# Spectral filter and two expert layers on one core: the image of x moved to partitions 0 to 46 and 64 to 110, with a rewritten start of the program

## The chip, the cores and the metric

The kernel runs on one core of a Trainium2 chip. The metric is the device time of one execution in microseconds (us); the time before is the median of three executions. The engines are PE (matrix products; its weight loads are listed as PEld), DVE and ACT (elementwise work), POOL (here mostly transfers and small copies) and SP (only issues transfers). A row that ends in q, such as SPq, is an engine's issue of a transfer. Each engine runs its own instructions strictly in program order.

## What is computed

```python
X = np.fft.rfft(x, axis=1)                 # x: 2 x 3008 x 256
Yr = Xr @ w_r - Xi @ w_i + b_r
Yi = Xr @ w_i + Xi @ w_r + b_i
Y  = soft_threshold(Yr, 0.01) + 1j * soft_threshold(Yi, 0.01)
y  = np.fft.irfft(Y, n=3008, axis=1)       # then 6016 tokens of 256
h  = y @ w_in;   y  = (h - tanh(h)) @ w_out            # 256 -> 2048 -> 256
h  = y @ w_in2;  out = (h * clip(h + 3, 0, 6) / 6) @ w_out2
```

## The kernel before

The transform of length 3008 = 47 x 64 is done in stages. Stage A (`dft_a`, chunks i = 0 to 15, eight for each batch) multiplies a chunk of x by a small constant matrix `amt`; ACT and DVE write the result back over the chunk (`dft_a_out`), and ACT issues its store to DRAM (`s<-xa` for batch 0, `s<-xb` for batch 1). Batch 0 lies whole in the tile `xa` (views `x0[0]` to `x0[7]`); batch 1 goes through a ring of three tiles `xb` (`x1`), each loaded by SP (`load_x`), used by PE, evicted, stored and then loaded again. Batch 0's first group of frequencies is also copied straight from `xa` into the ring tile `bi_all` by four transfers; the other groups are read back from DRAM (`load_bi`).

Stage B (`dft_b(j)`) multiplies a group of `bi_all` by a group of `bmt` (`load_bm(g)`, four frequencies in each, two used by each `dft_b`). ACT makes a high part `fh` and DVE a low part `fl` (`evict_b_*`). `linear(t)` is 24 PE instructions on `fh` and `fl`; DVE then does bias and threshold (`shrink(t)`: lines 349 to 351), ACT and DVE split the result into `sh` and `sl` (lines 357 and 361), and stage C (`dft_c`) goes back in frequency with the constants `cmH` and `cmL`, which POOL loads (`load_cm`, behind a small copy that waits for its last argument). A loop over t = 0 to 23 interleaves `linear(t)`, `dft_c(t - 2)`, `dft_b(t + 2)` and, while there are chunks left, one `dft_a` of batch 1. The order written in the code is the order that each engine keeps (`manual_schedule`).

The weights of the expert layers come as 64-bit floats (`raw`, three buffers) and are decoded to high and low parts on ACT and DVE by a generator, `w_steps`: each `w_step()` emits a step of it, in turn ACT lines 174 and 175, ACT line 184, DVE lines 177 and 187 with the next load (`w_load`), DVE line 192, DVE line 199, and for half of the weights DVE lines 203, 204 and then 206, 207. Five steps are run ahead of the loop, and six in each iteration from t = 2 to 9, fewer later, until 13 weights are decoded. `A0` is the number of chunks that go through stage A ahead of the loop. The expert layers, which fill the rest of the program, are not touched.

All transfers of SP and ACT share eight completion semaphores, which the tile framework hands out in turn: a transfer is not issued until the one that had its semaphore before it has landed. So at most eight transfers of these two queues are under way.

Of the kernel before, what the change touches and what calls it, by code (L numbers as in the profile page):

```python
# [18 lines left out]
N1 = 47  # L19
# [8 lines left out]
def dft_constants():  # L28
# [44 lines left out]

    am96 = np.zeros((96, 128))
    am96[0:94, 0:96] = am.reshape(94, 96)
    am96[0:94, 96:128] = am.reshape(94, K1, 4)[:, 0:8].transpose(0, 2, 1).reshape(94, 32)
    cm = cm.reshape(128, K1 * 128).astype(f)
# [11 lines left out]
def spectral_moe_kernel(ctx: ExitStack, tc: tile.TileContext, x, w_r, w_i, b_r, b_i,  # L89
# [25 lines left out]
    def split(hi, lo, src, lo_eng=None):  # L115
        act.activation(out=hi, in_=src, func=ACTF.Copy)  # L116
        (lo_eng or dve).tensor_tensor(out=lo, in0=src, in1=hi.bitcast(F32), op=ALU.subtract)  # L117
# [20 lines left out]

    A0 = 9
    NDEC = 13  # L140
# [95 lines left out]
    bias = ca.tile([128, 1, D], F32, name="bias")  # L236
    amt = ca.tile([96, 128], F32, name="amt")
    x1 = [wia.tile([128, 4, D], F32, tag=f"wo{5 + r}", name=f"xb{r}") for r in range(3)]
# [8 lines left out]
    def load_x(i):  # L247
        if i >= 16:
            return
        b, c = divmod(i, 8)  # L250
        if b == 0:
            v = x.rearrange("b s d -> (b s) d")[0:96 * 32].rearrange("(r j) d -> r j d", j=32)
            sp.dma_start(out=x0[c][0:96], in_=v[:, 4 * c:4 * c + 4, :])
        else:
            v = x[b].rearrange("(r j) d -> r j d", j=32)[:, 4 * c:4 * c + 4, :]
            for r0, r1 in ((0, 80), (80, 94)):
                sp.dma_start(out=x1[c % 3][r0:r1], in_=v[r0:r1])

# [5 lines left out]
    def dft_a(i, finish=True):  # L264
        b, c = divmod(i, 8)
        xt = (x1[c % 3] if b else x0[c])[0:96]
        m = 96 if b else 128
# [347 lines left out]
    with tc.manual_schedule():  # L615
# [12 lines left out]
        sp.dma_start(out=amt, in_=am)  # L628
        for i in range(8):
            load_x(i)  # L630
        warm = ca.tile([128, 256], F32, name="warm")
# [4 lines left out]
        for r in range(3):  # L636
            pool.memset(x1[r][64:96], 0.0)
        dve.memset(three, 3.0)
# [5 lines left out]
        load_bm(0)  # L644
        load_x(8)
        w_load()
        for k, w in enumerate((b_r, b_i)):
            sp.dma_start(out=bias[64 * k:64 * k + 64, 0, :],
                         in_=w.rearrange("(o d) -> o d", o=1).broadcast_to([64, D]))
        for i in range(A0):  # L650
            dft_a(i)
            if i == 5:
                for k in range(2):
                    split(lwH[:, k], lwL[:, k], lws[k])
            if i == 7:
                for k in range(GB):
                    sp.dma_start(out=bi_ring[0][:, k, :], in_=xa[96 + k:128:8])
                bi_t[0] = bi_ring[0]
        load_x(9)
        load_bi(1)  # L660
        load_bm(1)
        load_x(10)
        w_load()
        sp.dma_start(out=dmt, in_=dm)
        for _ in range(5):
            w_step()
        wa_cm.__exit__(None, None, None)
        wpool["r"] = ctx.enter_context(tc.tile_pool(name="wr", bufs=1, side="right", reuse_waits="tile"))
        for j in range(2):
            dft_b(j)  # L670
            evict_b_hi(j)
            evict_b_lo(j)
            evict_b_neg(j)
            if j == 0:
                load_cm(0, xf_t[0][0].bitcast(F32)[0:1, 0, 64:65])
        load_bi(2)
        NP = K1
        a_next = A0
        for t in range(NP):
# [21 lines left out]
            for _ in range(3 if t < 10 else 2):  # L701
                if t > 1 and ptr["dec"] < NDEC:
                    w_step()
# [11 lines left out]
            if t % 2 == 0:  # L715
                load_bm(t // 2 + 2)
                load_cm(t // 2 + 1, s_t[t][0].bitcast(F32)[0:1, 0, 0:1])
            load_x(11 + t)
            if t == 0:
# [3 lines left out]
            for _ in range(3 if t < 10 else 1 + t % 2):  # L723
                if t > 1 and ptr["dec"] < NDEC:
                    w_step()
# [124 lines left out]
```

## Time and profile before

| what | value |
|---|---|
| median of 3 executions (lowest, highest) | 1214.83 us (1214.05, 1216.38) |
| the profiled execution: time, span of its records | 1212.14 us, 1210.3 us |
| PE, DVE, ACT, POOL busy share of the span | 98%, 80%, 72%, 13% |
| granted clock of PE, mean | 0.993 |

The profiled execution lies 2.7 us under the median, within 2 us of the fastest run. PE's share is over the whole program; of the first tenth, the stages above, it says little.

### The profile page before, as it was taken

To read this page: it belongs to the slowest core of one execution; us is meant where nothing else is said; L and a number is where in the kernel's file an instruction comes from. 1 tells how busy PE (TensorE), PEld (TensorE's weight loads), DVE (VectorE), ACT (ScalarE), POOL (GpSimd) and SP (SyncE) were. 2 spreads that over 40 slices of the span, in tenths; PEclk is the share of its full clock that TensorE was granted. 3 is DMA by queue.
4 is the path that set the end of the run, shared out by engine and by line. 5 is a ranking of instruction groups with operands and counts; after the bars stand their busy time and mean duration, and the time that the engine had idled before them with its cause. 6 is when DMAs were issued, how large, how long until landed. Compare 5 with 4: busy or idle time off the path is not lost.

```text
span 1210.3 us, 20904 instructions
## 1 busy us (share of the span) xinstructions
PE 1185.4 (98%) x7832; PEld 1164.5 (96%) x7832; DVE 965.6 (80%) x1820; ACT 875.2 (72%) x1827; POOL 157.2 (13%) x162
## 2 busy tenths in 40 slices
PE   7989999999999999999999999999999999999998
PEld 5888989999999999999999999999999999999998
DVE  2589988888988888888777787878787878787875
ACT  2576678777777777777777677777777777776765
POOL 0100000203020110202021402011020202020200
PEclk8899999999999999999999999999999999999999
DMA  9996621112232223120105530101010101010000
GB/s 292 284 308 187 205 87 44 41 70 74 92 105 74 75 75 100 57 82 25 51 1 196 178 111 1 52 1 52 1 52 1 53 1 52 1 29 24 14 14 26
DMA packets 47797, 96.52 MB, mean 80 GB/s; under 512 B 4352, under 2 KB 27488, under 8 KB 47696
## 3 DMA queue, kind: packets, MB, share of 16 engines
q1 hardware_dynamic: 41728, 74.09, 19.2%
q0 software_dynamic: 4032, 14.68, 3.8%
q10 hardware_dynamic: 1936, 6.42, 1.4%
q8 instruction: 61, 1.00, 0.3%
q14 instruction: 40, 0.33, 0.1%
HBM read 58.22 MB, written 36.44 MB: 78 GB/s over the span
## 4 chain that ended last, share of the span: by engine, by line
PE 73%; DVE 11%; ACT 11%; DMA 2%; issue 2%; SPq 0%; ACTq 0%; DVEq 0%
PE acc L122 13%; PE acc L120 13%; PE acc L121 13%; PE al L120 6%; PE al L121 6%; PE al L122 6%; PE be L122 3%; PE be L121 3%; PE be L120 3%; ACT gh L116 3%; DVE g L447 3%; PE ga L405 2%; DVE gl L117 2%; PE ga L121 1%; PE ga L122 1%
## 5 line engine op out<-in xcount | busy, mean ns | idle before, releaser
L117 DVE TENSOR_TENSOR gl<-g,gh 128x376 fp32r<-128x376 f32 x509 | 292.2, 574 | 149.6 <-ACT gh L116 123.2
L116 ACT ACTIVATE gh<-g 128x376 fp32r<-128x376 f32 x509 | 263.4, 517 | 176.7 <-DVE g L450 91.5
L122 PE MATMUL acc<-wo,gl 128*128 128x256 f32 (+1 forms) x768 | 215.9, 281 | 0.0
L121 PE MATMUL acc<-wo,gh 128*128 128x256 f32 (+1 forms) x768 | 215.8, 281 | 0.0
L120 PE MATMUL acc<-wo,gh 128*128 128x256 f32 (+1 forms) x768 | 215.6, 281 | 0.0
L120 PE MATMUL acc<-gh,wo 128*128 128x376 f32 x512 | 173.2, 338 | 0.0
L122 PE MATMUL acc<-gh,wo 128*128 128x376 f32 x512 | 171.0, 334 | 0.0
L121 PE MATMUL acc<-gl,wo 128*128 128x376 f32 x512 | 170.7, 333 | 0.0
L121 PEld LDWEIGHTS acc<-wo,gh 128*128 128x128 f32 (+1 forms) x768 | 143.0, 186 | 0.0
L122 PEld LDWEIGHTS acc<-wo,gl 128*128 128x128 f32 (+1 forms) x768 | 142.9, 186 | 0.0
L120 PEld LDWEIGHTS acc<-wo,gh 128*128 128x128 f32 (+1 forms) x768 | 142.8, 186 | 0.0
L414 POOL TENSOR_TENSOR bmt<-bmt 128x376 f32<-128x376 f32 x60 | 73.4, 1224 | 445.5 <-ACT bmt L407 331.2
L450 DVE SCALAR_TENSOR_TENSOR g<-e,c 128x376 f32<-128x376 f32 x192 | 118.5, 617 | 12.2 <-ACT e L449 7.5
L449 ACT ACTIVATE e<-c,three 128x376 f32<-128x376 f32 x192 | 116.7, 608 | 7.7 <-DVE c L596 7.5
L447 DVE TENSOR_TENSOR g<-c,e 128x376 f32<-128x376 f32 x189 | 114.5, 606 | 5.9 <-ACT e L446 3.4
L430 POOL TENSOR_TENSOR cmL<-bmt,cmH 128x376 fp32r<-128x376 f32 x60 | 64.9, 1082 | 324.8 <-ACT cmH L425 324.8
L446 ACT ACTIVATE e<-c 128x376 f32<-128x376 f32 x189 | 97.6, 516 | 10.0 <-DVE c L596 9.8
L120 PEld LDWEIGHTS acc<-gh,wo 128*128 128x128 f32 x512 | 96.3, 188 | 0.0
L121 PEld LDWEIGHTS acc<-gl,wo 128*128 128x128 f32 x512 | 96.2, 188 | 0.0
L122 PEld LDWEIGHTS acc<-gh,wo 128*128 128x128 f32 x512 | 96.1, 188 | 0.0
L586 ACT ACTIVATE s<-be 128x376 f32<-128x376 f32 x127 | 61.8, 487 | 40.5 <-PE be L122 39.9
L120 PE MATMUL al<-cmH,wi 128*128 128x376 f32 x256 | 87.3, 341 | 2.1 <-ACT s L582 0.3
(173 smaller groups left out, 2831.2 us busy)
## 6 DMA issues: line engine op xcount, KB each, us to landing
raw<-in_moe_w_in_dram SPq DMA_DIRECT2D x16, 512.0 KB, 3.9
raw<-in_moe_w_out_dram SPq DMA_DIRECT2D x16, 512.0 KB, 4.2
w2id<-wout SPq DMA_DIRECT2D x8, 896.0 KB, 4.7
wi<-w2id POOLq DMA_DIRECT2D x8, 896.0 KB, 4.9
y1d<-y SPq DMA_DIRECT2D x32, 188.0 KB, 2.0
bmt<-y1d SPq DMA_DIRECT2D x8, 752.0 KB, 4.5
s<-co SPq DMA_DIRECT2D x23, 256.0 KB, 4.6
bi_all<-s SPq DMA_DIRECT2D x11, 512.0 KB, 5.1
```

The costliest lines, as they stand in the source:

```text
L116: act.activation(out=hi, in_=src, func=ACTF.Copy)
L117: (lo_eng or dve).tensor_tensor(out=lo, in0=src, in1=hi.bitcast(F32), op=ALU.subtract)
L120: pe.matmul(out=out_ap, lhsT=lh, rhs=rh, start=start, stop=False, **kw)
L121: pe.matmul(out=out_ap, lhsT=lh, rhs=rl, start=False, stop=False, **kw)
L122: pe.matmul(out=out_ap, lhsT=ll, rhs=rh, start=False, stop=stop, **kw)
L414: eng.tensor_tensor(out=out, in0=a, in1=b, op=ALU.subtract)
L430: (eng or dve).tensor_tensor(out=l, in0=OPS[nm][0], in1=h.bitcast(F32), op=ALU.subtract)
L446: act.activation(out=e, in_=src, func=ACTF.Tanh)
L447: dve.tensor_tensor(out=g, in0=src, in1=e, op=ALU.subtract)
L449: act.activation(out=e, in_=src, func=ACTF.Relu, bias=three)
L450: dve.scalar_tensor_tensor(out=g, in0=e, scalar=6.0, in1=src, op0=ALU.min, op1=ALU.mult)
L586: act.activation(out=s5, in_=be, func=ACTF.Copy)
```

## The change

x of batch 0 and 1 is laid out by the parity of its 32-row blocks: even blocks on partitions 0 to 46, odd ones on 64 to 110 (a 48th row of each parity is loaded for batch 0 and multiplied by zero rows of the constant). `amt` has 112 rows instead of 96, with zero rows between, and PE contracts over 112 partitions. A chunk of batch 0 is loaded by two transfers of 48 rows instead of one of 96; a chunk of batch 1 by four (32, 15, 32 and 15 rows) instead of two (80 and 14). What lies between must be finite, so DVE clears partitions 32 to 63 of each batch-0 chunk ahead of its load, and POOL clears two pieces of each `xb` tile instead of one.

The start of the program is rewritten: eight chunks instead of nine go through stage A ahead of the loop; on SP's queue the four copies into `bi_all` stand ahead of the bias, chunk 8 and the first raw weight; the split of the two filter matrices comes behind all of stage A; PE gets 11 products of a zero tile (`warm`) between stage A and stage B; no decode step runs ahead of the loop, and six run at t = 1. One chunk more goes through stage A in the loop (t = 0 to 7), and loads of x in the loop begin at t = 1.

```diff
-    A0 = 9
+    A0 = 8
-        if b == 0:
-            v = x.rearrange("b s d -> (b s) d")[0:96 * 32].rearrange("(r j) d -> r j d", j=32)
-            sp.dma_start(out=x0[c][0:96], in_=v[:, 4 * c:4 * c + 4, :])
-        else:
-            v = x[b].rearrange("(r j) d -> r j d", j=32)[:, 4 * c:4 * c + 4, :]
-            for r0, r1 in ((0, 80), (80, 94)):
-                sp.dma_start(out=x1[c % 3][r0:r1], in_=v[r0:r1])
+        v = x.rearrange("b s d -> (b s) d")[SEQ * b:SEQ * b + 64 * (47 if b else 48)]
+        v = v.rearrange("(n q j) d -> q n j d", q=2, j=32)[:, :, 4 * c:4 * c + 4, :]
+        for q in range(2):
+            if b == 0:
+                sp.dma_start(out=x0[c][64 * q:64 * q + 48], in_=v[q])
+                continue
+            for r0, r1 in ((0, 32), (32, 47)):
+                sp.dma_start(out=x1[c % 3][64 * q + r0:64 * q + r1], in_=v[q, r0:r1])
...
         for i in range(8):
+            dve.memset(x0[i][32:64], 0.0)
             load_x(i)
...
-        load_x(8)
-        w_load()
+        for i in range(A0):
+            dft_a(i)
+        for k in range(GB):
+            sp.dma_start(out=bi_ring[0][:, k, :], in_=xa[96 + k:128:8])
+        bi_t[0] = bi_ring[0]
         for k, w in enumerate((b_r, b_i)):
...
-        for i in range(A0):
-            dft_a(i)
-            if i == 5:
-                for k in range(2):
-                    split(lwH[:, k], lwL[:, k], lws[k])
-            if i == 7:
-                for k in range(GB):
-                    sp.dma_start(out=bi_ring[0][:, k, :], in_=xa[96 + k:128:8])
-                bi_t[0] = bi_ring[0]
+        load_x(8)
+        load_bi(1)
+        w_load()
         load_x(9)
-        load_bi(1)
         load_bm(1)
+        sp.dma_start(out=dmt, in_=dm)
         load_x(10)
         w_load()
-        sp.dma_start(out=dmt, in_=dm)
-        for _ in range(5):
-            w_step()
+        load_cm(0, bi_ring[0][0:1, 0, 0:1])
+        for k in range(2):
+            split(lwH[:, k], lwL[:, k], lws[k])
+        for _ in range(11):
+            p = bank("h")
+            pe.matmul(out=p[:, 0:256], lhsT=warm[:, 0:128], rhs=warm, start=True, stop=True)
...
-                if t > 1 and ptr["dec"] < NDEC:
+                if t > 0 and ptr["dec"] < NDEC:
...
-            load_x(11 + t)
+            if t > 0:
+                load_x(10 + t)
```

**Place 1: DVE at the very start.** Before, DVE clears `warm` first:

```order
L632 MEMSET warm 128x256
L638 MEMSET three 128x1
L284 COPY xa<-be 128x512
L284 COPY xa<-acc 128x512
L284 COPY xa<-ga 128x512
```

In the change eight clears of 32 partitions by 1024 elements stand ahead of it; PE's first four instructions read `warm`, and stage A stands behind them:

```order
L633 MEMSET xa 32x1024 x8
L636 MEMSET warm 128x256
L643 MEMSET three 128x1
L287 COPY xa<-be 128x512
L287 COPY xa<-acc 128x512
```

**Place 2: SP's queue behind the first group of `bmt`.** Before, up to the second group of `bmt`:

```order
L257 DMA xb_98<-in_x_dram 80x1024
L257 DMA xb_98<-in_x_dram 14x1024
L158 DMA raw<-in_moe_w_in_dram 128x2x256
L648 DMA bias<-in_b_r_dram 64x256
L648 DMA bias<-in_b_i_dram 64x256
L657 DMA bi_all<-xa 128x1x256 x4
L257 DMA xb_99<-in_x_dram 80x1024
L257 DMA xb_99<-in_x_dram 14x1024
L297 DMA bi_all<-s_0_60 128x4x256
L620 DMA bmt<-in_bm_dram 128x512
```

In the change, from the four copies on; ahead of them stands only what loads batch 0, the filter matrices and the first group of `bmt`, and between the first row and the second group of `bmt` (the row behind the last one here, after two more pieces of `xb_99`) there are 16 transfers:

```order
L653 DMA bi_all<-xa 128x1x256 x4
L656 DMA bias<-in_b_r_dram 64x256
L656 DMA bias<-in_b_i_dram 64x256
L260 DMA xb_98<-in_x_dram 32x1024
L260 DMA xb_98<-in_x_dram 15x1024
L260 DMA xb_98<-in_x_dram 32x1024
L260 DMA xb_98<-in_x_dram 15x1024
L300 DMA bi_all<-s_0_60 128x4x256
L160 DMA raw<-in_moe_w_in_dram 128x2x256
L260 DMA xb_99<-in_x_dram 32x1024
L260 DMA xb_99<-in_x_dram 15x1024
```

**Place 3: ACT in two iterations of the loop.** Before (from the high part of `fh` on; the first group of rows is one iteration, of which the decode's lines 174 and 175 come behind `sh` and the second write of `fl`):

```order
L315 ACTIVATE fh<-al 128x4x128
L316 ACTIVATE fh<-al 128x4x64
L357 ACTIVATE sh<-ly 128x512
L327 ACTIVATE fl<-fl 128x4x64
L174 ACTIVATE ws<-raw 128x512
L175 ACTIVATE ws<-raw 128x512
L184 ACTIVATE wi_627<-ws 128x896
L286 ACTIVATE xb_100<-be 96x512
L286 ACTIVATE xb_100<-al 96x512
```

In the change the generator is one step further at the same place, so those two stand at the end of the iteration ahead, in front of its `co` and `fh`, and line 184 (here 186) follows `fl` at once:

```order
L289 ACTIVATE xb_98<-ga 96x512
L289 ACTIVATE xb_98<-al 96x512
L290 DMA s_1_61<-xb_98 96x1024
L176 ACTIVATE ws<-raw 128x512
L177 ACTIVATE ws<-raw 128x512
L382 ACTIVATE co<-acc 128x512
L318 ACTIVATE fh<-be 128x4x128
L319 ACTIVATE fh<-be 128x4x64
L360 ACTIVATE sh<-ly 128x512
L330 ACTIVATE fl<-fl 128x4x64
L186 ACTIVATE wi_669<-ws 128x896
```

## Rows read from the trace of the kernel before

**Rows 1.** The profile's page: PE over the span.

```profile
PE 1185.4 (98%) x7832; PEld 1164.5 (96%) x7832; DVE 965.6 (80%) x1820; ACT 875.2 (72%) x1827; POOL 157.2 (13%) x162
```

**Rows 2.** Busy time by stretch; then PE's granted clock, DMA share, GB/s.

```profile
20.00:25.00 5.00, 1.68 (x4) 1.24 (x5) 2.03 (x4) 1.11 (x3) 0.00 (x0) 0.64 1.03 409
35.00:40.00 5.00, 5.00 (x31) 5.00 (x31) 0.91 (x2) 1.29 (x3) 0.00 (x0) 0.65 1.27 276
```

**Rows 3.** Chain of waits, first 60 us: start, length, what.

```profile
26.41 7.83 DMA bi_all<-xa
```

**Rows 4.** Timeline, first 24 us: start, length, engine, line.

```profile
0.75 2.72 POOL L637 MEMSET xb<- 32x1024 f32 x3 [0.29 <-POOLq L833]
0.87 0.27 DVE L632 MEMSET warm<- 128x256 f32 x1 [0.87 <-PEq L833]
1.20 1.22 PE L635 MATMUL al<-warm 128*128 128x256 f32 x2 [1.20 <-DVE three L638]
5.35 1.10 PE L273 MATMUL al<-xa,amt 96*128 96x256 f32 x4 [0.61 <-DMA xa<-in_x_dram]
8.13 0.37 ACTq L287 DMA_DIRECT2D s<-xa  x1
17.51 1.89 PE L273 MATMUL acc<-xa,amt 96*128 96x256 f32 x8
23.43 4.15 SPq L657 DMA_DIRECT2D bi_all<-xa  x4
```

**Rows 5.** Timeline, 35 to 54 us: the first `linear` groups.

```profile
35.17 0.56 PE L120 MATMUL acc<-lwH,fh 128*128 128x256 f32 x1
39.58 1.06 PE L308 MATMUL al<-bmt,bi_all 128*128 128x128 f32 x8
42.02 0.47 PE L120 MATMUL acc<-lwH,fh 128*128 128x256 f32 x1
45.27 0.69 DVE L349 TENSOR_TENSOR ly<-acc,bias 128x512 f32<-128x512 f32 x1 [2.21 <-PE acc L122]
47.51 0.47 PE L120 MATMUL acc<-lwH,fh 128*128 128x256 f32 x1
53.70 0.47 PE L120 MATMUL acc<-lwH,fh 128*128 128x256 f32 x1
```

**Rows 6.** Transfers of the first 80 us: KB, median us from issue to landing.

```profile
s<-xa ACTq DMA_DIRECT2D x8, 384.0 KB, 6.3
xb<-in_x_dram SPq DMA_DIRECT2D x8, 320.0 KB, 7.8
bmt<-in_bm_dram SPq DMA_DIRECT2D x5, 256.0 KB, 7.5
bias<-in_b_r_dram SPq DMA_DIRECT2D x1, 64.0 KB, 4.2
```

**Rows 7.** DVE's timeline in the loop; waits before a row in brackets.

```profile
50.75 0.69 DVE L349 TENSOR_TENSOR ly<-acc,bias 128x512 f32<-128x512 f32 x1 [2.22 <-PE acc L122]
58.27 0.68 DVE L349 TENSOR_TENSOR ly<-acc,bias 128x512 f32<-128x512 f32 x1
68.44 0.51 DVE L177 TENSOR_SCALAR raw<-raw 128x512 uint32<-128x512 uint32 x1 [1.05 <-ACT ws L174]
71.80 0.68 DVE L349 TENSOR_TENSOR ly<-acc,bias 128x512 f32<-128x512 f32 x1
105.37 0.68 DVE L349 TENSOR_TENSOR ly<-acc,bias 128x512 f32<-128x512 f32 x1
```

**Rows 8.** Waits of all engines, 38 to 130 us: total, times, longest.

```profile
DVE raw L177 <- ACT ws L174: 5.2, 5, 1.0
DVE fl L322 <- ACT fh L316: 1.1, 4, 0.6
```

**Rows 9.** ACT's timeline at one decode step of the loop.

```profile
67.75 0.66 ACT L174 ACTIVATE ws<-raw 128x512 f32<-128x512 f32 x1
68.88 0.94 ACT L184 ACTIVATE wi<-ws 128x896 fp32r<-128x896 f32 x1
```

More of the change, by code (lines that the diff above doesn't have):

```diff
@@ L72, in round_r @@
         return u.view(f)
-    am96 = np.zeros((96, 128))
-    am96[0:94, 0:96] = am.reshape(94, 96)
-    am96[0:94, 96:128] = am.reshape(94, K1, 4)[:, 0:8].transpose(0, 2, 1).reshape(94, 32)
+    am96 = np.zeros((112, 128))
+    for q in range(2):
+        aq = am[:, q].reshape(N1, K1, 4)
+        am96[64 * q:64 * q + N1, 0:96] = aq.reshape(N1, 96)
+        am96[64 * q:64 * q + N1, 96:128] = aq[:, 0:8].transpose(0, 2, 1).reshape(N1, 32)
     cm = cm.reshape(128, K1 * 128).astype(f)
@@ L236, in spectral_moe_kernel @@
     bias = ca.tile([128, 1, D], F32, name="bias")
-    amt = ca.tile([96, 128], F32, name="amt")
+    amt = ca.tile([112, 128], F32, name="amt")
     x1 = [wia.tile([128, 4, D], F32, tag=f"wo{5 + r}", name=f"xb{r}") for r in range(3)]
@@ L250, in load_x @@
         b, c = divmod(i, 8)
-        if b == 0:
-            v = x.rearrange("b s d -> (b s) d")[0:96 * 32].rearrange("(r j) d -> r j d", j=32)
-            sp.dma_start(out=x0[c][0:96], in_=v[:, 4 * c:4 * c + 4, :])
-        else:
-            v = x[b].rearrange("(r j) d -> r j d", j=32)[:, 4 * c:4 * c + 4, :]
-            for r0, r1 in ((0, 80), (80, 94)):
-                sp.dma_start(out=x1[c % 3][r0:r1], in_=v[r0:r1])
+        v = x.rearrange("b s d -> (b s) d")[SEQ * b:SEQ * b + 64 * (47 if b else 48)]
+        v = v.rearrange("(n q j) d -> q n j d", q=2, j=32)[:, :, 4 * c:4 * c + 4, :]
+        for q in range(2):
+            if b == 0:
[3 more added lines that the diff above has]
+                sp.dma_start(out=x1[c % 3][64 * q + r0:64 * q + r1], in_=v[q, r0:r1])
     def flush_stores():
@@ L265, in dft_a @@
         b, c = divmod(i, 8)
-        xt = (x1[c % 3] if b else x0[c])[0:96]
+        xt = (x1[c % 3] if b else x0[c])[0:112]
         m = 96 if b else 128
@@ L636, in spectral_moe_kernel @@
         for r in range(3):
-            pool.memset(x1[r][64:96], 0.0)
+            for q in range(2):
+                pool.memset(x1[r][64 * q + 32:64 * q + 64], 0.0)
         dve.memset(three, 3.0)
@@ L673, in spectral_moe_kernel @@
             evict_b_neg(j)
-            if j == 0:
-                load_cm(0, xf_t[0][0].bitcast(F32)[0:1, 0, 64:65])
         load_bi(2)
@@ L723, in spectral_moe_kernel @@
             for _ in range(3 if t < 10 else 1 + t % 2):
-                if t > 1 and ptr["dec"] < NDEC:
+                if t > 0 and ptr["dec"] < NDEC:
                     w_step()
```

## Prediction

> **What bounds the kernel now.** I read the page first: PE is busy 98% of the span [rows 1], so a change at the start is worth only what it shifts the whole rest by. The chain of waits and the stretches show where PE does wait. Three stretches matter. First, stage A: PE begins at 5.35 us, when the first chunk has landed, and ends its eighth chunk at 17.51 + 1.89 = 19.40, in 14.05 us without a gap worth naming [rows 4]. Second, a wait for transfers: the four copies into `bi_all` are issued from 23.43 on [rows 4], and the chain stands on the last of them from 26.41 to 34.24 [rows 3]; `linear(0)` begins at 35.17 [rows 5]. [...] Third, from `shrink(2)` at 50.75 on, DVE carries the decode: eight iterations take 105.37 - 50.75 = 54.6 us, a pair of them 71.80 - 58.27 = 13.5 [rows 7], while PE needs 47.51 to 53.70 = 6.2 for one [rows 5], 12.4 for two. The waits say where DVE itself stands idle there: five times 1.04 us at line 177 for ACT's line 174, four waits of 1.1 in all for `fh` [rows 8].
>
> So the end moves by two things: when `linear(1)` begins (42.02), and how long DVE takes from there.
>
> **The change, part by part: the start.** DVE's eight clears stand ahead of `warm`, and PE's four products of `warm` ahead of stage A. The trace has no clear of this shape on DVE. 256 elements took 0.27 us, POOL's three clears of this very shape 2.72, or 0.91 each [rows 4]. Four times 0.27 is the upper bound, 1.08; the lower one, if a long clear ran at twice that rate, is 0.6. I take 1.05, since 0.27 for 256 is already 1.05 ns for an element. Eight take 8.4: `warm` is cleared from 9.3 us (was 0.87), 8.4 later. PE needs 5.35 - 0.61 - 1.20 = 3.5 us for the four products (its low clock: 0.88 each, against 14.05 / 32 = 0.44 in stage A) [rows 4]. It starts stage A at 9.6 + 3.5 = 13.2 and ends it at 27.2, where the old one ended at 19.4.
>
> x costs nothing there. It is issued from 2 us on, behind the first clear, and stage A took 0.39 MB every 1.75 us in the old order without waiting [rows 4]; now all but the last chunk have eight microseconds more. The last chunk's two transfers use the semaphores of the first two stores of `s`, so they go only when these have landed. The first store comes 8.13 - 5.35 = 2.8 us after stage A's start [rows 4], so at 16, the second at 17.7; with 3.5 to 6.3 us to land, the median of such a store [rows 6], the last chunk is there by 23.5 to 26.5 and is wanted at 25.4. I take no wait, 1 us at worst. [...]
>
> The last eviction, 0.8 us behind PE, ends at 28.0; the four copies are issued from 28.1 (was 23.43). Ahead of them there is less: chunk 8, a raw weight and the bias, 1.0 MB, now stand behind. The old last copy took 7.8 us to land [rows 3]; I take 4.5, near the bias rows' 4.2 [rows 6], from an issue at 30.4: 34.9. So `linear(0)` begins at about 35.2, where it did before. [...]
>
> Then comes what is late next: `dft_b(2)`, old start 39.58 [rows 5], needs the second groups of `bi_all` and `bmt`. The latter is now the 17th transfer from the first copy on. With eight semaphores that is two full rounds of landing: issue at 28.1 + 2 x 4.6 = 37.3, landing at 41.5 with 4.2 more, at 44.8 with the 7.5 of `bmt`'s own row [rows 6], at 39 if the queue is as empty as it was never in this trace. By bytes: some 4.0 MB are to be moved between 28.1 and then; at 276 to 409 GB/s [rows 2] that is 10 to 14.5 us, 38 to 42.6. I take 41.5, which is **+1.9 us** for `linear(1)` (bounds -0.9 and +5.2, the latter with PE idle from 38.3 to 44.8, in which its clock falls as it did between 20 and 25 us [rows 2], for another 1.5).
>
> **The loop.** At t = 1 DVE has six decode steps more. It had 50.75 - 45.27 = 5.5 us between two `shrink`s [rows 5, 7] and now has what an iteration of the old loop had, its own rows, six steps and the wait at line 177: half of 13.5 [rows 7], 6.8, so **+1.3**. From t = 2 on, the generator is one step ahead at the same place. ACT's lines 174 and 175 then come at the end of the iteration before, so line 177 finds its input ready: 1.05 goes in each pair, and with it the wait of (1.1 - 0.6) / 3 = 0.17 at `fl` [rows 8], which came of ACT's lateness there. In its place line 192 of that iteration waits for ACT's line 184, which can start where line 174 did, at 67.75, and ends 0.94 later [rows 9], at 68.7. DVE was ready for line 177 at 68.44 - 1.05 = 67.4 [rows 7], and that line and 187 take it some 1.1, to 68.5: a wait of 0.2 to 0.3. So 13.5 becomes 12.6 a pair, just over PE's 12.4; four pairs give **-3.6**. The first of them had another 0.6 for `fh` behind stage C [rows 8], which DVE, now later than PE, doesn't see: **-0.6**. At t = 10 the fifth wait at line 177 goes too: **-1.0**. One step less is left at the end: **-0.3**. Sum for the loop -4.2; if ACT falls behind elsewhere, the waits only move, and it is +1.3 instead.
>
> Chunk 8 leaves the start and each chunk of the loop comes one iteration later, under PE's 6.2. The ring of `xb` costs something: its load is four transfers instead of two, and store, load and use have to fit three iterations, now 18.9 us instead of 20.3, with 6.3 and 7.8 us to land [rows 6]: 14.1 plus 1.7 for PE, 2.5 for ACT's turn, and some 1 for issue is 19.3. I take **+0.3**, between nothing and 2.5 (five uses at 0.5).
>
> Sum: +1.9 + 1.3 - 3.6 - 0.6 - 1.0 - 0.3 + 0.3 = **-2.0 us**. On the profiled execution that is 1212.1 - 2.0 = 1210.1; the median of the runs stands 2.7 above it, so I give 1214.83 - 2.0 = 1212.8. 0.2% is 2.4 us here, about what a measurement of this kernel can tell from no change.
>
> **The rivals.** *Cheap clears.* If 1024 elements take 0.7 us, stage A starts 2.8 us earlier, `linear(0)` ends at 35.5, the second group of `bmt` lands at 38.7, and the +1.9 becomes -0.9: -4.8, 1210.0. For it: POOL's 0.91; against: DVE's own row. It is also the time if the transfers behind 28 us land faster than I take.
>
> *The ring binds.* If store and load of `xb` take their medians and issue takes 2 us more, five iterations are paced by it at up to 0.7 us over my 6.3, and most of the loop's gain goes: +1.9 - 4.2 + 3.5 = +1.2, 1216.0. For it: the sum of 19.3 above. Against: PE hardly waits for x in the old loop, where the ring had 1.4 us more.
>
> *The late constants* (the other side). If the second group of `bmt` takes 7.5 us from its issue, PE stands until 44.8 and comes back at low clock: 5.2 + 1.5 - 4.2 + 0.3 = +2.8, 1217.6. It decides from a landing at 44.4 on, given the clock; at 43.5 without it the change is worth nothing. For it: that is the row's median; against: that median was taken with larger transfers in the queue ahead of it.
>
> **How the numbers follow.** My forecast 0.42, cheap clears or fast landing 0.22, the ring 0.16, late constants 0.20. The forecast spans -4 to 0, so 0.18 of it is faster by over 0.2% and 0.24 within. The ring is within (0.15) or slower (0.01), the late constants slower (0.18) or within (0.02). Faster 0.40, same 0.41, slower 0.19. The range reaches from 1208.5 (cheap clears with the loop's gain in full) to 1218 (late constants).
>
> **What would show it.** In the changed profile: eight clears of about 1.05 us on DVE, with `warm` at 9.3; PE's first chunk at 13.2 and last at 27.2; the first copy into `bi_all` issued at 28; `linear(0)` at 35 at granted clock near 1; a wait of PE of about 3 us for `bmt` ahead of `dft_b(2)`; in the loop no wait at line 177 (179 there) but one at t = 1, and pairs of `shrink` 12.6 apart. Wrong would be: clears of half the length, `dft_b(2)` that waits for nothing or until 44, pairs still 13.5 apart, or PE waiting for `xb`.

## The result, and the profile after

The changed kernel takes 1227.11 us (median of 4 runs, 1226.34 to 1227.36), the kernel before, measured beside it, 1214.78: ratio 1.0098, 95% interval 1.0085 to 1.0111, that is 12 us slower. The forecast was 1212.8, its range ended at 1218. Of all the runs below, one of e15 (3426.70 us, its profiled one) and one of before beside e5 to e9 (4087.02 us) are left out of the ratios as slow. The profiled execution of after took 1227.24 (span 1225.5), 15.1 more than that of before, which lay 2.7 under its median.

Busy shares of the page, for [rows 1]: PE has 22 instructions more and is busy 6.3 us longer; the other 9 us of the span are waits.

```profile
PE 1191.7 (97%) x7854; PEld 1172.2 (96%) x7854; DVE 970.5 (79%) x1827; ACT 877.8 (72%) x1828; POOL 160.8 (13%) x165
```

The kernel after by stretches, for [rows 2] (columns as there: busy times, then granted clock, DMA share, GB/s). Between 45 and 50 us PE does nothing at all, and in the stretches beside it its granted clock is 0.56 and 0.53.

```profile
10.00:15.00 5.00, 5.00 (x15) 4.13 (x16) 0.00 (x0) 0.35 (x1) 0.00 (x0) 1.00 1.05 220
35.00:40.00 5.00, 2.92 (x15) 2.57 (x16) 0.69 (x1) 1.55 (x4) 0.15 (x1) 0.76 1.05 228
40.00:45.00 5.00, 4.69 (x23) 4.49 (x22) 0.96 (x2) 1.02 (x3) 0.00 (x0) 0.56 1.08 268
45.00:50.00 5.00, 0.00 (x0) 0.00 (x0) 1.54 (x3) 0.00 (x0) 0.00 (x0) 0.78 0.81 173
50.00:55.00 5.00, 4.48 (x15) 3.69 (x16) 1.29 (x2) 2.10 (x5) 0.81 (x2) 0.53 0.80 251
```

The timeline of after up to the third pair's first transform, for [rows 4, 5].

```profile
1.02 0.91 DVE L633 MEMSET xa<- 32x1024 f32 x1 [1.02 <-PEq L837]
...
9.57 0.27 DVE L636 MEMSET warm<- 128x256 f32 x1
...
13.47 1.14 PE L276 MATMUL al<-xa,amt 112*128 112x256 f32 x4
...
25.67 1.95 PE L276 MATMUL acc<-xa,amt 112*128 112x256 f32 x8
...
28.42 4.81 SPq L653 DMA_DIRECT2D bi_all<-xa  x4
...
33.89 0.68 PE L311 MATMUL ga<-bmt,bi_all 128*128 128x128 f32 x4 [1.52 <-DMA bi_all<-xa]
35.18 0.71 PE L311 MATMUL ga<-bmt,bi_all 128*128 128x128 f32 x4 [0.61 <-DMA bi_all<-xa]
36.86 0.68 PE L311 MATMUL al<-bmt,bi_all 128*128 128x128 f32 x4 [0.96 <-DMA bi_all<-xa]
38.47 1.22 PE L311 MATMUL al<-bmt,bi_all 128*128 128x128 f32 x4 [0.93 <-DMA bi_all<-xa]
39.35 0.56 PE L122 MATMUL acc<-lwH,fh 128*128 128x256 f32 x1
...
43.03 0.35 SPq L623 DMA_DIRECT2D bmt<-in_bm_dram  x1
...
50.52 2.04 PE L311 MATMUL be<-bmt,bi_all 128*128 128x128 f32 x8 [5.83 <-DMA xb<-in_x_dram]
```

Read it downwards: clears, stage A and the issue of the copies stand within half a microsecond of where the forecast put them. Then each copy lets PE go on for one piece of `dft_b` only, 1.3 to 1.7 us apart, the last at 38.47 (forecast 34.9). `linear(0)` runs from 39.35, at a granted clock of 0.56 (40 to 45 us), where [rows 5] had 35.17. The second group of `bmt` is issued at 43.03 (forecast 37.3) and `dft_b(2)` starts at 50.52, 10.9 us later than before. The row gives the wait to `xb`; by the code, `dft_b(2)` reads the second groups of `bi_all` and `bmt`. The chain of waits of after, same place, shows the former landing at 37.63 + 7.14 = 44.77:

```profile
37.63 7.14 DMA bi_all<-s
44.79 5.70 DMA xb<-in_x_dram
```

So from 44.8 on it is `bmt` that is missing. The waits of SP's queue show when it lands: the next issue that takes over its semaphore stands until 50.43 and goes at 50.45, 7.4 us after the issue of `bmt`.

```profile
SPq L300 <- DMA bmt<-in_bm_dram: 1.3, 1, 1.3
```

DVE's timeline of after, `shrink` at t = 0, 1, 2, 4 and 5, for [rows 5, 7], and what PE and SP do in the last gap:

```profile
44.73 0.69 DVE L352 TENSOR_TENSOR ly<-acc,bias 128x512 f32<-128x512 f32 x1 [3.40 <-PE acc L124]
58.29 0.69 DVE L352 TENSOR_TENSOR ly<-acc,bias 128x512 f32<-128x512 f32 x1 [3.44 <-PE acc L124]
65.26 0.68 DVE L352 TENSOR_TENSOR ly<-acc,bias 128x512 f32<-128x512 f32 x1
...
70.40 7.64 SPq L260 DMA_DIRECT2D xb<-in_x_dram  x4
...
77.43 0.68 DVE L352 TENSOR_TENSOR ly<-acc,bias 128x512 f32<-128x512 f32 x1
80.48 1.07 PE L276 MATMUL al<-xb,amt 112*96 112x256 f32 x4 [1.97 <-DVE raw L179]
86.86 0.69 DVE L352 TENSOR_TENSOR ly<-acc,bias 128x512 f32<-128x512 f32 x1 [1.90 <-PE acc L124]
```

Here t = 1 is 13.0 late. The first pair after t = 2 takes 77.43 - 65.26 = 12.17, as the loop's terms said it would; then one iteration takes 9.4. SP's four loads of a chunk stretch from 70.40 to 78.04 there. The row puts PE's wait at 80.48 to a DVE row; chunk 12, which PE wants next, is the likelier cause, and the experiments on batch 1 bear it out. Its first two pieces go at 70.40 and 70.86, so its buffer is free; the third goes only at 77.18, when the store of chunk 10, which lies in another buffer, has landed (issue of that store, and the wait of SP's queue from 70 to 78 us):

```profile
70.01 0.31 ACTq L290 DMA_DIRECT2D s<-xb  x1
...
SPq L260 <- DMA s<-xb: 5.8, 1, 5.8
```

At t = 10 `shrink` stands at 120.09, where [rows 7] had 105.37: 14.7 late.

The waits of after, all engines, 38 to 130 us, for [rows 8]: the wait for line 174 (now 176) has shrunk from 5.2 to 1.8, and the small new one at ACT's next line, forecast as 0.2 to 0.3 each, is there.

```profile
PE be L311 <- DMA xb<-in_x_dram: 5.8, 1, 5.8
...
DVE raw L179 <- ACT ws L176: 1.8, 2, 1.0
...
DVE wi L194 <- ACT wi L186: 1.0, 4, 0.3
```

### The profile page after: what moved, and what is told of

It reads as the page before. It is cut to its first block, busy times and chain, and to the rows that moved or that the text cites. A ratio compares the mean times of both kernels' runs of the same rounds, so it can differ in the third digit from the quotient of the medians.

```text
span 1225.5 us, 21012 instructions
## 1 busy us (share of the span) xinstructions
PE 1191.7 (97%) x7854; PEld 1172.2 (96%) x7854; DVE 970.5 (79%) x1827; ACT 877.8 (72%) x1828; POOL 160.8 (13%) x165
## 4 chain that ended last, share of the span: by engine, by line
PE 74%; ACT 10%; DVE 10%; DMA 3%; issue 2%; SPq 1%; ACTq 0%
PE acc L122 12%; PE acc L124 12%; PE acc L123 12%; PE al L122 6%; PE al L123 6%; PE al L124 6%; PE be L124 3%; PE be L123 3%; PE be L122 3%; ACT gh L118 3%; DVE g L450 2%; PE ga L408 2%; DVE gl L119 2%; PE ga L123 1%; PE ga L124 1%
```

## The experiments

Theories when the first four were sent: the delay is the clears and the place of `bmt` on SP's list (first), the transfers of the new layout by themselves (second), or the new order whatever the layout (third). All results first; "late at t" is `shrink`'s start in the profile against the kernel with the order alone, which itself stood at 51.26 (t = 1) and 109.47 (t = 10); e2 has the order of before, against which it is 12.5 and 21.7 late. The time against before is the ratio, less one, times the median of before measured beside it.

| kernel | median us | ratio [95%] | against before, us | late at t = 1 | late at t = 10 |
|---|---|---|---|---|---|
| order alone (e1) | 1214.68 | 0.9997 [0.9988, 1.0007] | -0.4 | 0 | 0 |
| layout alone (e2) | 1230.63 | 1.0129 [1.0093, 1.0166] | +15.7 | 6.5 | 17.6 |
| after | 1227.11 | 1.0098 [1.0085, 1.0111] | +11.9 | 7.0 | 10.6 |
| after, `warm` first (e3) | 1226.30 | 1.0092 [1.0077, 1.0107] | +11.2 | 6.5 | 11.4 |
| after, `bmt` early (e4) | 1226.71 | 1.0097 [1.0082, 1.0112] | +11.8 | 3.2 | 11.4 |
| after, ring of 4 (e5) | 1225.77 | 1.0104 [1.0087, 1.0122] | +12.6 | 7.5 | 12.3 |
| order, batch 1 new (e7) | 1219.27 | 1.0041 [1.0028, 1.0055] | +5.0 | -0.3 | 4.8 |
| order, batch 0 new (e8) | 1223.05 | 1.0077 [1.0062, 1.0092] | +9.3 | 6.3 | 6.8 |
| after, batch 1 in two loads (e9) | 1223.48 | 1.0081 [1.0066, 1.0096] | +9.8 | 5.8 | 6.2 |
| e3, two queues (e13) | 1223.74 | 1.0070 [1.0055, 1.0085] | +8.5 | 4.4 | 9.9 |
| e9, `warm` first, two queues (e14) | 1221.74 | 1.0054 [1.0040, 1.0068] | +6.6 | 4.0 | 5.0 |
| order, batch 0 in two loads (e16) | 1218.34 | 1.0028 [1.0017, 1.0038] | +3.4 | 3.2 | 3.8 |
| the same by parity (e17) | 1218.60 | 1.0031 [1.0019, 1.0042] | +3.8 | 4.0 | 3.5 |
| order, batch 1 in one load (e11) | 1214.68 | 1.0003 [0.9994, 1.0012] | +0.4 | -1.4 | -1.9 |
| the same, `bmt` early (e15, e18) | 1207.90, 1206.89 | 0.9944 [0.9927, 0.9960] | -6.8 | -8.5 | -8.7 |

**e1, the order alone.** Layout, loads and constant of before in the new order, no clears.

```
-            dve.memset(x0[i][32:64], 0.0)
             load_x(i)
```

> The new order with x where it was before (96-row loads, no clears on DVE). Theory 1 (the clears delay stage A by 8 us, and the second group of bmt, which stands 17th in the queue, then costs two rounds of landing): stage A runs from 5.3 to 19.4 us, the copies into bi_all are issued at about 20.3, 8 us earlier than in the change; bmt stands 13th, is issued at about 33 and lands at 39 to 40, so linear(1) begins at 42 to 43, as before the change, and with the shorter loop the time is 1209 to 1214. Theory 2 (the short transfers of 48, 32 and 15 rows slow the queue by themselves): as fast or faster, 1205 to 1212. Theory 3 (the new order of SP's queue costs the time whatever the layout): linear(1) still at 48 or later, 1219 or more.

**e2, the layout alone.** The order of before with the new loads, constant and clears.

> The old order with the new layout (clears on DVE, 48-row loads, four transfers for a chunk of batch 1). Theory 1: stage A 8 us later, and what hangs on it too; bmt's second group stands well ahead in the old queue, so linear(1) is 8 to 10 us late and the pairs of iterations stay at 13.5 us: 1222 to 1226. Theory 2: the same or worse, 1225 to 1232. Theory 3: little, 1215 to 1219.

The order by itself costs nothing and wins nothing; the layout by itself costs all of it, so the third theory falls. (Whether it costs more than in after isn't shown: two of its four runs took 1227 us and two 1234 to 1236, and the profile is of one of the latter.) The trace of the order alone shows why it wins nothing. Its stage A begins at 5.91, its copies are issued at 22.63, and then `dft_b(2)` starts at 43.86 (timeline below, then two `shrink`s), 4.3 later than in [rows 5]: there too `bmt`'s second group, issued at 33.71, comes last (the row names a raw weight, but SP's next issue on its semaphore waits for `bmt` until 43.77; e18 below moves it).

```profile
43.86 2.04 PE L308 MATMUL be<-bmt,bi_all 128*128 128x128 f32 x8 [5.79 <-DMA raw<-in_moe_w_out_dram]
...
70.41 0.68 DVE L349 TENSOR_TENSOR ly<-acc,bias 128x512 f32<-128x512 f32 x1
77.52 0.68 DVE L349 TENSOR_TENSOR ly<-acc,bias 128x512 f32<-128x512 f32 x1
```

From t = 2 to 10 it needs 109.47 - 58.24 = 51.2 us, where [rows 7] had 54.6: the loop's gain is real, 3.4 us. It doesn't pay all that was lost ahead of it: this kernel is 7.5 us late at t = 2 (58.24 after 50.75), 4.1 at t = 10 and 2.1 at t = 20 (154.84 after 152.76). Its profile ends 3.0 after that of before (1213.3 after 1210.3); by the medians, under which the profile of before lies by 2.7, the two are equal.

**e3, `warm` first.** The clear of `warm` ahead of the eight clears of x.

```
         sp.dma_start(out=amt, in_=am)
+        warm = ca.tile([128, 256], F32, name="warm")
+        dve.memset(warm, 0.0)
         for i in range(8):
             dve.memset(x0[i][32:64], 0.0)
             load_x(i)
-        warm = ca.tile([128, 256], F32, name="warm")
-        dve.memset(warm, 0.0)
```

> The change with the clear of warm ahead of the eight clears of x on DVE, nothing else. Theory 1: PE's first products run from 1.3 us, stage A begins at about 6.2 instead of 13.5 and is then paced by loads and clears at about 1.8 us a chunk; the copies go out at 21.5 to 23 and everything behind is 5 to 7 us earlier: 1219 to 1222. Theory 2: x arrives too slowly at half height, stage A waits for it and ends at 25 or later: 1224 to 1227. Theory 3: 1222 to 1227, since the queue behind the copies is as it was.

Stage A begins at 6.73 and not at 13.47, and the time is the same: the first theory's larger half falls. The timeline shows the hole at chunk 6, and the waits of SP's queue (first 30 us) its cause.

```profile
23.30 1.59 PE L276 MATMUL al<-xa,amt 112*128 112x256 f32 x4 [3.81 <-DMA xa<-in_x_dram]
```

```profile
SPq L257 <- DMA s<-xa: 6.0, 1, 6.0
```

Sixteen loads no longer fit eight semaphores: the last ones wait until a store of stage A has landed, are issued up to 20.9, and the copies go at 29.48, a microsecond later than in after. So two delays of equal length lie side by side: the clears, and behind them the loads. The prediction had the last loads behind stores and took no wait of PE from that, which holds in after; taking away the first shows what it hid.

**e4, `bmt` early.** The second group of `bmt` issued right behind the first.

```
         load_bm(0)
+        load_bm(1)
...
-        load_bm(1)
```

> The change with the load of bmt's second group moved up to right behind that of the first, nothing else. Theory 1: dft_b(2) then waits for the second group of bi_all alone, which landed at about 44.8: it begins at 44.8 instead of 50.5, PE's idle time there falls from 5.8 us to below 1, its clock falls less: 5 to 7 us less, 1220 to 1222. Theory 2: bytes and packets are the same, so the second group of bi_all comes as much later: 1225 to 1227. Theory 3: as theory 1, and at least 6 us.

```profile
46.99 1.54 PE L311 MATMUL be<-bmt,bi_all 128*128 128x128 f32 x8 [1.91 <-DMA xb<-in_x_dram]
...
63.64 1.14 PE L311 MATMUL ga<-bmt,bi_all 128*128 128x128 f32 x8 [3.06 <-DMA bmt<-in_bm_dram]
```

`dft_b(2)` comes 3.5 us earlier, and at the third group PE waits again: by t = 10 nothing is left of it (11.4 late, after 10.6). The list as a whole is late; moving one of its entries forward moves the wait to another.

**e5, a fourth buffer for batch 1.** The list's delay or the ring's?

```
+    ring = x1 + [din0]
-                sp.dma_start(out=x1[c % 3][64 * q + r0:64 * q + r1], in_=v[q, r0:r1])
+                sp.dma_start(out=ring[c % 4][64 * q + r0:64 * q + r1], in_=v[q, r0:r1])
```

> The kernel after, with four buffers for batch 1's chunks in the place of three (the tile `din0`, which nothing uses until later, is the fourth; its zero rows are cleared by GpSimd like the others). The computation is whole. Ring theory (in the loop a chunk's load waits until its buffer is free, and that is what stops the first part of the net at 77.43 to 86.86): the load of chunk 12 no longer waits for the store of chunk 9, the stop of 9.4 us between the two net operations shrinks towards 6.3, and the time falls to 1222 to 1224.5. Queue theory (SP's list as a whole runs late: twice as many transfers for each chunk, one of eight semaphores each, whichever buffer they go to): the stop moves by less than 1 us or appears at another place, 1226 to 1228. Start theory (all 12 us are lost before the loop's second step, the loop only carries them): 1226 to 1228 as well, but the last net operation of the loop stands where it did, at 181.

The gap between t = 4 and 5 falls from 9.4 to 8.1 (77.87 to 86.00), and one of 10.2 opens between t = 6 and 7 (92.46 to 102.71). So it isn't buffers that are missing, as the queue's theory has it; the time, 1225.8, lies between the bands of the two. Here the row of the stop names chunk 12's load itself, and its third piece waits for a store again (issued at 70.46, landed at 76.44):

```profile
81.15 1.07 PE L277 MATMUL al<-xb,amt 112*96 112x256 f32 x4 [1.85 <-DMA xb<-in_x_dram]
```

**e7 and e8, one batch at a time.** Both in the new order, with two stationary constants.

```
+        at_ = amt2 if b else amt
-                pe.matmul(out=pv[:, u, :], lhsT=amt[:, 0:m], rhs=xt[:, 2 * g + u, :], start=True, stop=True)
+                pe.matmul(out=pv[:, u, :], lhsT=at_[:, 0:m], rhs=xt[:, 2 * g + u, :], start=True, stop=True)
```

> The new order; batch 0 as before (rows in order on partitions 0 to 95, one load of 96 rows a chunk, no clears), batch 1 as in the kernel after (by parity, four loads a chunk). A second stationary constant, loaded once by GpSimd, holds the weights for batch 1. The computation is whole. Start theory (clears and the 48-row loads of batch 0 make the 12 us): stage A, the copies and the second group of `bmt` stand as in the kernel with the order alone (5.9, 22.6, issue 33.7), and the time is 1214 to 1217. Queue theory (four transfers for a chunk of batch 1 keep SP's list late in the loop): the first net operations are as early as with the order alone, but the chain waits for a chunk at the fifth to the eighth step, the lead is lost there, and the time is 1222 to 1227.

> The new order; batch 0 as in the kernel after (by parity, eight clears, two loads of 48 rows a chunk), batch 1 as before (rows in order, two loads a chunk of 80 and 14 rows). A second stationary constant, loaded once by GpSimd, holds the weights for batch 1. The computation is whole. Start theory: the late start stays (copies 28.4, second group of `bmt` issued near 42), and the time is 1224 to 1227. Queue theory: the start is as late, since only four transfers less stand ahead of `bmt`, which is issued 2 to 3 us earlier; but the loop does not wait for chunk 12 any more and catches up 3 to 8 us of the 14.5, 1217 to 1223.

The two halves are lost at two places, and nearly add: 4.8 and 6.8 us at t = 10, 10.6 in after (by time 5.0 and 9.3, which is 2.4 more than after's 11.9; each time lies between the bands of its two theories). Batch 1's half is lost in the loop (-0.3 at t = 1). The stop stands where after has it; timeline of e7, t = 4 and 5:

```profile
70.14 0.68 DVE L358 TENSOR_TENSOR ly<-acc,bias 128x512 f32<-128x512 f32 x1
80.32 0.69 DVE L358 TENSOR_TENSOR ly<-acc,bias 128x512 f32<-128x512 f32 x1 [1.34 <-PE acc L128]
```

10.2 us against 7.1 with the order alone. Batch 0's half is lost before t = 1 and carried. Its kernel issues the second group of `bmt` at 38.95, four earlier than after, yet `dft_b(2)` starts at 49.63, and its row names `bmt`: by the chain of waits of e8 that transfer takes 10.6 us.

```profile
38.95 10.58 DMA bmt<-in_bm_dram
49.63 2.05 PE L318 MATMUL be<-bmt,bi_all 128*128 128x128 f32 x8 [5.19 <-DMA bmt<-in_bm_dram]
```

**e9, batch 1 in two loads of 48 rows a chunk.**

```
+        s0 = SEQ * b - 64 * b
+        v = x.rearrange("b s d -> (b s) d")[s0:s0 + 64 * 48]
...
+            sp.dma_start(out=(x1[c % 3] if b else x0[c])[64 * q:64 * q + 48], in_=v[q])
-            for r0, r1 in ((0, 32), (32, 47)):
-                sp.dma_start(out=x1[c % 3][64 * q + r0:64 * q + r1], in_=v[q, r0:r1])
```

> The kernel after with batch 1 in two loads of 48 rows a chunk in the place of four of 32 and 15: the load begins one row of each parity earlier (the last rows of batch 0), and a second stationary constant, loaded once by GpSimd, has the weights moved by one partition and a row of zeros for it. The computation is whole. Same layout, same halves of partitions, half as many transfers. If the number of transfers counts (queue theory): the second group of `bmt` is issued 2 to 4 us earlier than 43.0, the chain does not stop for chunk 12, 1217 to 1223, close to the kernel with only batch 0 changed. If the layout itself is slow, each load reaching half of the partitions: chunks land as late as before, 1225 to 1227. Start theory: 1225 to 1227.

The stop in the loop goes (76.20 to 82.72, 6.5 us), the time is that of the kernel whose batch 1 has the old layout. So batch 1 costs by the number of its transfers, four a chunk, and not by its place in the partitions. By time it is 1223.5, half a microsecond over the band that this theory gave; the start's part was larger than thought.

**e13 and e14, batch 0 through two queues.** GpSimd issues the second parity's loads.

```
-                sp.dma_start(out=x0[c][64 * q:64 * q + 48], in_=v[q])
+                (pool if q else sp).dma_start(out=x0[c][64 * q:64 * q + 48], in_=v[q])
```

> The kernel with the clear of `warm` first, and with the second parity's load of each chunk of batch 0 (to partitions 64 to 111) issued by GpSimd's queue in the place of SP's. Same layout, same clears, same transfers; SP's list is eight transfers shorter ahead of the weights, none of its last loads waits for a store of stage A, and both halves of the partitions are written at the same time. The computation is whole. Half-height theory (one 48-row transfer at a time reaches half of the partitions, and that holds the loads at 193 to 220 GB/s with the DMA engines full): x comes at 235 GB/s or more from 5 to 15 us. Semaphore theory (SP's list, with its last loads behind stores, is what makes stage A and the copies late): the rate of x stays at 195 to 220, but the last chunk comes near 18 and stage A runs without a hole. Under both the copies are issued near 24 to 26 in the place of 29.5, the second group of `bmt` near 37 to 39, and the time is 1219 to 1222. If the 48-row loads cost the time by something else (GpSimd's issue, the clears), the copies stay at 28 or later and the time at 1225 to 1228.

> All three pieces put right with the layout kept: the clear of `warm` first, batch 0's second parity loaded by GpSimd's queue, batch 1 in two loads of 48 rows a chunk with a second stationary constant. The computation is whole. If the loss of 12 us is the sum of a late start (6.3 us, from batch 0's 48-row loads on one queue) and of four transfers a chunk in the loop (3 us), with some 2 us that follow, this kernel stands near the order alone: 1215 to 1218. If the layout costs in another way, 1220 to 1224.

The copies come at 26.40 and 25.96 instead of 29.48, and 2.7 and 3.2 us are won: SP's shorter list counts (the expectation had 1219 to 1222 for e13; it took 1223.7). But x comes no faster. e14 by stretches:

```profile
5.00:10.00 5.00, 2.41 (x6) 1.99 (x7) 4.25 (x6) 1.61 (x2) 4.74 (x7) 1.00 1.04 197
10.00:15.00 5.00, 5.00 (x15) 3.73 (x14) 1.28 (x2) 0.87 (x2) 2.00 (x3) 1.00 1.04 200
```

The DMA engines are full (1.04) and move 197 to 200 GB/s. The order alone, same stretches, moves more at the same share:

```profile
5.00:10.00 5.00, 4.09 (x10) 3.36 (x11) 0.30 (x1) 1.88 (x2) 0.00 (x0) 1.00 1.04 237
10.00:15.00 5.00, 5.00 (x25) 4.40 (x24) 1.82 (x4) 1.78 (x3) 0.00 (x0) 1.00 1.04 236
```

So two queues that write both halves at once are no remedy, against what I expected of that theory, and e14 stays 6.6 us over before.

**e16 and e17, what slows the loads of batch 0.** Old partitions, new order; first only halved, then halved by parity.

```
-            sp.dma_start(out=x0[c][0:96], in_=v[:, 4 * c:4 * c + 4, :])
+            for r0 in (0, 48):
+                sp.dma_start(out=x0[c][r0:r0 + 48], in_=v[r0:r0 + 48, 4 * c:4 * c + 4, :])
```

> The new order with the old layout, and each chunk of batch 0 in two loads of 48 rows (rows 0 to 47, then 48 to 95) in the place of one of 96: same partitions, same addresses, no clears; batch 1 as before. The computation is whole. Semaphore theory (sixteen loads of x on SP's list, the last of them behind stores of stage A): the rate stays at 237 to 250 GB/s from 5 to 15 us, but the last chunk waits for a store, the copies go from 22.6 to 25 to 28, the time is 1217 to 1222. If 48-row loads are themselves slow, whatever they write and read: 195 to 220 GB/s. If neither counts (it is the layout in memory): as the order alone, copies at 22 to 23.5 and 1213.5 to 1216.

> As the last, but the two loads of a chunk read the rows of one parity each (48 rows of 4 KB, 64 KB apart in memory in the place of 32) and write partitions 0 to 47 and 48 to 95, without a gap and without clears; batch 1 as before with its own stationary constant (GpSimd loads it). The computation is whole. If the address step of the source makes the loads slow: 195 to 220 GB/s from 5 to 15 us where the split by rows has more. If the destination does (48 partitions at 0 and at 64): the rate is that of the split by rows. Time: that of the split by rows in the second case, 1217 to 1222; one or two us more in the first.

Stretch 5 to 10 us of e16, of e17, and of e8, which adds the gap between the halves and the clears:

```profile
5.00:10.00 5.00, 4.82 (x11) 3.87 (x12) 0.69 (x1) 1.88 (x2) 0.00 (x0) 1.00 1.04 238
```

```profile
5.00:10.00 5.00, 4.93 (x19) 4.25 (x20) 1.00 (x2) 2.48 (x3) 0.00 (x0) 1.00 1.02 252
```

```profile
5.00:10.00 5.00, 0.10 (x1) 0.10 (x1) 4.09 (x7) 1.28 (x1) 0.00 (x0) 1.00 1.04 199
10.00:15.00 5.00, 5.00 (x16) 4.16 (x17) 0.00 (x0) 0.60 (x1) 0.00 (x0) 1.00 1.05 195
```

Neither half the size nor the parities' address step slows the loads: 238 and 252 GB/s. The destination does, partitions 0 to 47 and 64 to 111 in the place of 0 to 47 and 48 to 95: 195 to 199, also from 10 us on, when the clears are over. Nor is it the stores of stage A, which begin earlier in some kernels: from 4 to 8 us, before the first store of any kernel (8.13), the nine kernels with the gap moved 178 to 215 GB/s and the seven without it 239 to 266, at a DMA share of 0.98 to 1.07. Sixteen loads where there were eight cost 3.4 us for another reason, SP's semaphores: they wait for stores again (SP's queue in e16, first 30 us), and the copies go at 26.81.

```profile
SPq L254 <- DMA s<-xa: 8.6, 3, 4.5
```

The rate is not one figure: 195 to 200 GB/s in e8 and e14 (5 to 15 us), with one queue or two, but 211 to 222 in after and e9 with the same loads of batch 0. The runs show that the destination slows the loads; why it does, they don't show.

**e11 and e15, fewer transfers.** The order and layout of e1, with batch 1 in a single load of 96 rows that begins two rows earlier, its weights in a second constant moved by two; then `bmt` early as well.

```
+        s0 = SEQ * b - 64 * b
+        v = x.rearrange("b s d -> (b s) d")[s0:s0 + 96 * 32].rearrange("(r j) d -> r j d", j=32)
+        sp.dma_start(out=(x1[c % 3] if b else x0[c])[0:96], in_=v[:, 4 * c:4 * c + 4, :])
```

> The new order with the old layout, and batch 1 in one load of 96 rows a chunk in the place of two of 80 and 14: it begins two rows earlier, and a second stationary constant (GpSimd loads it once) has the weights two partitions further on. No zero rows, no clears. The computation is whole. If the number of transfers on SP's list sets when the second group of `bmt` and the loop's chunks come (3 us for two transfers a chunk more, by the kernels with batch 1 in four or two), one fewer for each chunk brings `bmt` 1 to 2 us earlier and shortens the stop at chunk 12 by 1 to 2: 1210 to 1213. If only the short transfers of the split layout cost, 1214 to 1215.5.

> The same with the second group of `bmt` issued right behind the first. The computation is whole. The wait of 5.8 us of the third pair's first transform for that group goes; where the order alone gave back what it won, by the next transfers on the list, it does so here too, by less: 1208 to 1212 if the list has room now, 1212 to 1215 if the gain is given back at the third group or at chunk 12, as in the kernel with the same edit on the new layout.

> The new order with the old layout, batch 1 in one load of 96 rows a chunk, and the second group of `bmt` right behind the first, once more, for a trace of its start. The computation is whole. The first measurement gave 1208.6, so 1207 to 1210; the third pair's first transform no longer waits for `bmt`, linear(1) ends 4 to 6 us earlier than with the order alone, and the stop before chunk 12's products is at most 2 us longer than there (it was 7.1 between the two net operations).

Fewer transfers alone give nothing by time (0.4 us, within the interval): 1.9 us at t = 10 are lost again behind it. With `bmt` early too the kernel beats both: 0.9944 in each of two measurements, 6.8 us under before. e18 is the same kernel as e15, measured again; its timeline:

```profile
36.96 1.13 PE L309 MATMUL be<-bmt,bi_all 128*128 128x128 f32 x8 [0.31 <-DMA bi_all<-s]
...
42.74 0.69 DVE L350 TENSOR_TENSOR ly<-acc,bias 128x512 f32<-128x512 f32 x1 [2.35 <-PE acc L125]
```

`dft_b(2)` hardly waits, t = 1 comes at 42.74 in the place of 51.26, and this time the gain stays (8.7 at t = 10). The edit that was worth 0.1 us on the long list of after is worth 7 on the short one. Whether the order alone, with two loads a chunk, would gain as much by it, no run shows.

## Why the prediction was wrong, point by point

**Clears, stage A, issue of the copies: right.** `warm` at 9.57 (forecast 9.3), stage A 13.47 to 27.6 (13.2 to 27.2), copies from 28.42 (28.1). The clears last 0.91 but start every 1.07 us, so the 1.05 taken fits the pace. Cheap clears, the first rival, falls. That PE's first four products run at a low clock no run shows: the granted clock is 1.00 in before (0 to 5 us) and in after (9.9 to 13.4 us), where they take 13.47 - 9.90 = 3.6 us, and why that is twice the time of stage A's products is open.

**"x costs nothing there": right, and misleading.** In after nothing waits for x. But its loads alone would put the copies at 29.48 (e3), so the start can't be had back by the clears.

**The copies, 4.5 us from issue to landing, 34.9: the first step that failed.** The last was issued at 32.06, not 30.4, and landed at 38.4, after 6.4 us. They don't land side by side: four pieces came 1.3 to 1.7 us apart, in the order alone too (28.00, 29.30 and on to 32.48). The DMA view of after, 28 to 40 us, 0.3 us to a figure, shows their rate:

```profile
GB/s 447 416 434 393 403 423 355 410 328 304 283 201 116 116 123 96 96 96 96 99 96 96 96 106 212 219 191 263 263 222 294 263 266 222 239 273 297 164 143 201
```

First the last stores at 400, then some 3.5 us at 96 to 123 while the copies have the queue. Over the whole stretch from 28.1 to 50.4 us the rate was 224 GB/s, not the 276 to 409 of the prediction's sum by bytes. A granted clock near 1 for `linear(0)` failed with it: PE waits between the pieces, 0.76 and 0.56 were granted (35 to 40 and 40 to 45 us), and `linear(0)` took 44.69 - 39.35 = 5.3 us. The forecast's 38.3 for its end was 35.2 and an estimated 3.1, the time of `linear(1)` in [rows 5] (47.51 - 42.02, less 42.02 - 39.58); that the 11 products of `warm` ahead of it bring `linear(0)` to 3.1, no run shows. They ended at 32.37, and the clock was 1.00 from 30 to 35 us.

**"Issue 37.3, landing 41.5" for the second group of `bmt`, +1.9: the step that decided.** It was issued at 43.03, and what waited for it started at 50.52; `dft_b(2)` was 10.9 us later than in [rows 5], and `linear(1)`, at 55.03 in the place of 42.02, 13.0 and not 1.9. I had counted two rounds of landing at 4.6 us for a list of 17. In the list stand the copies, two bias rows that take SP 1.1 us each, and eight loads for two chunks, 1.98 and 3.96 us of SP's time; and the landing took 7.4, or 8.9 and 10.6 where it was issued earlier (e9 at 40.47, e8 at 38.95), not 4.2. An earlier issue therefore brings `bmt` hardly earlier: 49.4 and 49.5 instead of 50.4. The DMA engines are full there (share 1.05 and 1.08 from 35 to 45 us in after), so the bytes under way ahead of it may count as well as the places on the list; which of the two sets the landing, the runs don't tell apart. The upper bound of 5.2 was that of "late constants", the right rival with far too small a price: its worst case was a landing at 44.8, it was 50.4. The 1.5 it adds for a fallen clock was an estimate of mine, which no run shows by itself; `dft_b(2)` and stage A behind it took 55.03 - 50.52 = 4.5 us in after, at a granted clock of 0.53 (50 to 55 us), where [rows 5] had 42.02 - 39.58 = 2.4. The order alone has the same wait (5.8 us, +6.0 at t = 1) without any of the new layout. So this term was mis-sized for the order by 4, and the layout adds 7 to it.

**The loop, -4.2: about right with the order alone, nothing in after.** t = 1 to 2 took 1.5 us more (forecast 1.3), the wait at line 177 fell from 5.2 to 1.8. With the order alone t = 2 to 10 gained 3.4 of the 4.2 counted there (3.6 + 0.6), unevenly: the first pair took 12.17 (forecast 12.6), the other three 12.5 to 13.3. In after t = 2 to 10 took 120.09 - 65.26 = 54.8 us, where [rows 7] had 54.6: the stops for chunks use the gain up.

**The ring, +0.3 with 2.5 at most: mis-sized, and not by the ring.** Four loads a chunk cost 5.0 us alone and 2.6 on top of batch 0's; a fourth buffer gives none of it back (e5), two loads in the place of four do (e9). The term counted when a buffer comes free; what came late was a semaphore, eight for all transfers of the two queues.

The 12 us follow, in steps that were each measured: the order 0 by the medians; batch 0 in sixteen loads 3.4; by parity 0.4 more, within the intervals; the gap between the halves, with clears and slower loads, 5.5 more; four loads a chunk for batch 1 2.6 more (the intervals of e8 and after just overlap, but e7 has 5.0 clear of noise). The share of the clears and that of the slower loads within the 5.5 are not told apart: each hides the other. Past t = 10 some more is lost: e8 and e9, 6.8 and 6.2 us late there, are 7.6 and 6.6 late at t = 20 (162.44 and 161.46 after 154.84), and their profiles end 8.5 and 7.5 after that of the order alone (spans 1221.8 and 1220.8, and 1213.3). Its cause stays open.

## What to carry to other kernels

Count a queue's list, not only its bytes: where a completion semaphore has to come free before the next transfer goes, one load cut in two delays what stands behind it on the list (in e16 the copies went at 26.81, with the order alone at 22.63), and the delay shows at a transfer that the change didn't touch. A forecast that puts a transfer n places down a list should take each entry's own time on the issuing queue (1.1 us for a bias row here) and the landing times seen under load (7.4 us for the second group of `bmt` in after, 10.6 in e8), not the best one (4.0, the first group in e17). And an edit that starts one transfer earlier is worth trying again after the list has been shortened: here it went from nothing to 7 us.

## What was not expected of the hardware

Loads to partitions 0 to 47 and 64 to 111 moved 178 to 215 GB/s from 4 to 8 us with the DMA engines full (share 0.98 to 1.07), loads of the same size to 0 to 47 and 48 to 95 239 and 246 (e16, e17). Copies from four partitions held the rate at about 96 GB/s, whichever kernel (before, after, e1, e3, e9, e17, e18). In after the DMA share was 0.29 between 31.6 and 35.2 us, 1.03 from 25 to 30 and 1.05 from 35 to 40. The 256 KB of a group of `bmt` took 4.0 us to land at the least (first group, e17), 7.4 in after and 10.1 to 11.0 in e1, e8, e11 and e14 (second group, at a DMA share of 1.01 to 1.08 from 35 to 45 us).
